# Attention and a gated feed-forward on one core: the reciprocals of the softmax sums go through DRAM and a broadcasting DMA instead of 64-fold copies and transpositions

## The chip, the cores and the metric

The kernel runs on one core of a Trainium2 chip. Its time is the device time of one execution, in microseconds (us). A core has a matrix engine (PE, with its weight loads shown apart as PEld), a vector engine (DVE), a scalar engine (ACT), a general engine (POOL), a queue engine that here only issues transfers (SP), and 16 DMA engines. The engines run side by side; each takes its own instructions in order and waits on semaphores for the others.

## The reference, cut to what matters

```python
def _attn_ref(q, k, v):                       # (8, 8, 576, 64) each
    scores = np.matmul(q, k.transpose(0, 1, 3, 2)) / np.sqrt(64)
    mask = (pos[:, None] // 64) >= (pos[None, :] // 64)
    scores = np.where(mask, scores, -1e9)
    scores = scores - np.max(scores, axis=-1, keepdims=True)
    attn = np.exp(scores)
    attn = attn / (np.sum(attn, axis=-1, keepdims=True) + 1e-09)
    return np.matmul(attn, v)

def _moe_ref(x, w_in, w_out):                 # x: 4608 x 512, from the 8 heads of each batch
    h = x @ w_in                              # 4608 x 2048
    sp = np.maximum(h, 0.0) + np.log1p(np.exp(-np.abs(h)))
    return (h * erf(sp)) @ w_out              # 4608 x 512
```

## The kernel before, in words

There are 8 batches of 8 heads, 64 heads in all, numbered n. Accuracy is kept by splitting operands into a high and a low part, so that nearly every product is three matrix multiplications.

**Attention.** The main loop has one step for each head and four more (`for n in range(N + 4)`). A step emits, merged evenly: the loads of head n+3 (`load_qk`: a load to `st` on SP, a load into `qk` on POOL's queue, two copies from SBUF to SBUF on SP, then two subtractions on POOL, L312 and L313, for the low parts); the row maxima of head n+2 (`maxes`, L324 on PE, L327 on DVE, then a transposition and L356 on ACT); the probabilities of head n (`probs`, L370 and L371 on PE, L375 and L381 on ACT, L382 on DVE); and for each pair of heads the unnormalised outputs `usb` and the sums `rs` (`pv`, L414 to L440). In the second step of every four, v of the next four heads is loaded; in the third it is split (`prep_v`, L276 to L292).

**Normalising.** Two pairs of heads, four heads, make a quad; there are 16 quads, two to a batch. For each quad `normalise` turns the sums so that queries lie on partitions (L453, six small products into `rt`), takes the reciprocals (L454, `ri`), and then, for each of the two pairs, copies each reciprocal 64 times along a row (L462, `rw`, on ACT), transposes these rows back on PE (L467, five products for a pair, into two PSUM banks `rb`) and multiplies `usb` by them on DVE (L469). The product is split into two parts (L470 on ACT, L471 on POOL) and written to `x_d` in DRAM by SP (L472). All of it is emitted in one step of the main loop, the one with n = 1 modulo 4.

**Feed-forward.** d_ff is 16 chunks of 128. The first six (`F1`) go through `moe1` while attention runs: units of two chunks over 256 tokens, up (L154), the gate (L123 to L137) and down (L164). They read `x_d` back (L187) when a batch is ready (`ready_at`). What is left of them follows after attention, and then come the other ten chunks over 512 tokens at a time. The weights come as the words of float64 and are converted by DVE, ACT and POOL (L94 to L108).

**Order.** The kernel is written in this order, but a scheduler takes each instruction by its place in the program as a priority and issues it on its engine where its own model finds the operands ready. So multiplications of `moe1`, which stand late in the program, fill places between those of attention. Until the first `x_d` is read, each step also emits ten products that nobody reads (`warm`, L510).

PSUM has eight banks. `bank` gives four of them in turn to scores, probabilities, sums, outputs and the reciprocals (`ps_a`) once the feed-forward has begun.

## Time and profile before

| | us |
|---|---|
| median of three runs | 1399.85 |
| lowest and highest of them | 1387.88, 1400.71 |
| the profiled execution, first to last instruction | 1407.0 |
| PE busy in it | 1273.8 (91%) |
| PE loading weights | 1026.1 (73%) |
| DVE busy | 1013.9 (72%) |
| ACT busy | 793.2 (56%) |
| POOL busy | 602.1 (43%) |

The profiled execution is 0.5% longer than the median of the runs. Busy time is the time in which an engine had an instruction under way; "idle before" is the time that an engine stood before the instructions of a group, with what ended it. The profile names instructions by line and by what they write and read. Windows of time (from the span's start) give the busy time of each engine in a stretch, the clock that PE was granted (1.00 is full speed) and the share of the 16 DMA engines. Attention lasts from the start to about 760 us, what is left of the first six chunks to about 850 us, and the other ten chunks to the end.

### The profile page before, as it was taken

The page shows a single profiled execution, that of the slowest core. Times are in us where ns is not written, and L with a number is a line of the kernel's source. Part 1 is how long each engine was busy: PE and PEld are TensorE (multiplying, and loading weights), DVE is VectorE, ACT ScalarE, POOL GpSimd, SP SyncE. Part 2 cuts the span into 40 slices and gives each one's busy share as a digit, 9 for nine tenths or more (in the row PEclk, how much of TensorE's full clock was granted, in tenths as well). Part 3 has the DMA queues.
Part 4 walks back from the last instruction along what each step waited for, and adds up shares of the span by engine and source line. Part 5 has one row for each costly group of instructions (what it writes and reads, how often), then busy time and mean ns, then how long its engine had stood idle before and what let it go on. Part 6 is the DMA issues. An engine that isn't in the chain of part 4 may idle for free. (4 is left out here: it accounts for less than half of the span.)

```text
span 1407.0 us, 21952 instructions
## 1 busy us (share of the span) xinstructions
PE 1273.8 (91%) x8198; PEld 1026.1 (73%) x8198; DVE 1013.9 (72%) x1525; ACT 793.2 (56%) x1493; POOL 602.1 (43%) x454
## 2 busy tenths in 40 slices
PE   3798789989899898999889898779999999999998
PEld 1455567777777787777777787568888888888887
DVE  5768997788878788788697648996555555564654
ACT  1456566667666676667567455544444454445453
POOL 3757665445554554544445424562222222222221
PEclk9879899999999999999999899899999999999999
DMA  8557655757657576566623542302211311321110
GB/s 228 135 125 204 173 156 137 185 154 193 179 129 207 146 196 175 152 161 177 174 81 137 188 164 95 130 0 78 102 60 68 113 60 60 108 72 61 60 61 30
DMA packets 89370, 179.95 MB, mean 128 GB/s; under 512 B 8540, under 2 KB 27292, under 8 KB 89264
## 3 DMA queue, kind: packets, MB, share of 16 engines
q1 hardware_dynamic: 79280, 159.41, 38.1%
q0 software_dynamic: 9344, 18.97, 6.1%
q8 instruction: 65, 1.06, 0.3%
q10 hardware_dynamic: 640, 0.17, 0.1%
q14 instruction: 41, 0.34, 0.1%
HBM read 112.29 MB, written 37.75 MB: 107 GB/s over the span
## 5 line engine op out<-in xcount | busy, mean ns | idle before, releaser
L130 DVE SCALAR_TENSOR_TENSOR m_r<-m_r 128x512 f32<-128x512 f32 x288 | 232.9, 809 | 229.3 <-ACT m_r L128 225.8
L137 POOL TENSOR_TENSOR m_gl<-m_r,m_gh 128x512 fp32r<-128x512 f32 x144 | 195.5, 1357 | 443.7 <-ACT m_gh L136 359.2
L136 ACT CAST m_gh<-m_r 128x512 fp32r<-128x512 f32 x144 | 89.2, 619 | 251.9 <-DVE m_r L135 251.7
L154 PE MATMUL m_h<-xh,whi 128*128 128x256 f32 (+1 forms) x648 | 213.3, 329 | 17.3 <-DVE m_r L135 17.3
L128 ACT ACTIVATE m_r<-m_r,c 128x512 f32<-128x512 f32 x288 | 207.9, 722 | 11.0 <-ACT m_r L128 0.4
L154 PE MATMUL m_h<-xl,whi 128*128 128x256 f32 (+1 forms) x648 | 211.1, 326 | 0.3 <-DMA xl<-x_d 0.3
L154 PE MATMUL m_h<-xh,wlo 128*128 128x256 f32 (+1 forms) x648 | 211.1, 326 | 0.0
L327 DVE TENSOR_REDUCE mx<-s 64x1 f32<-64x288 f32 (+4 forms) x384 | 167.9, 468 | 56.4 <-PE s L324 53.9
L375 ACT ACTIVATE p<-t 128x288 f32<-128x288 f32 (+4 forms) x384 | 143.1, 388 | 97.9 <-PE t L371 76.2
L164 PE MATMUL o<-whi,m_gh 128*128 128x512 f32 x432 | 173.8, 403 | 6.7 <-ACT ob L209 4.3
L164 PE MATMUL o<-wlo,m_gh 128*128 128x512 f32 x432 | 173.8, 402 | 0.0
L382 DVE TENSOR_TENSOR pl<-p,ph 128x832 f16<-128x832 f32 (+1 forms) x128 | 158.5, 1240 | 18.0 <-ACT ph L381 17.8
L312 POOL TENSOR_TENSOR qk<-st,qk 64x576 fp32r<-64x576 f32 x64 | 103.2, 1613 | 157.5 <-PE s L324 55.9
L154 PEld LDWEIGHTS m_h<-xh,whi 128*128 128x128 f32 x648 | 126.6, 195 | 37.8 <-DVE m_r L135 21.9
L164 PE MATMUL o<-whi,m_gl 128*128 128x512 f32 x432 | 153.0, 402 | 0.2 <-POOL m_gl L137 0.2
L370 PE MATMUL t<-qk 69*128 69x288 f32 (+4 forms) x384 | 136.0, 355 | 12.6 <-DVE mx L327 7.0
L324 PE MATMUL s<-qk 68*128 68x256 f32 (+3 forms) x384 | 126.6, 362 | 14.3 <-DVE mx L327 8.7
L313 POOL TENSOR_TENSOR qk<-st,qk 64x576 fp32r<-64x576 f32 x64 | 111.3, 1739 | 65.5 <-DMA qk<-qk 61.7
L154 PEld LDWEIGHTS m_h<-xl,whi 128*128 128x128 f32 x648 | 126.5, 195 | 15.8 <-DMA xl<-x_d 0.6
L154 PEld LDWEIGHTS m_h<-xh,wlo 128*128 128x128 f32 x648 | 126.9, 196 | 9.4
L371 PE MATMUL t<-qk 128*128 128x288 f32 (+4 forms) x384 | 129.8, 339 | 0.0
L123 ACT ACTIVATE m_r<-m_h,c 128x512 f32<-128x512 f32 x144 | 98.8, 686 | 50.5 <-PE m_h L154 48.7
(84 smaller groups left out, 2499.1 us busy)
## 6 DMA issues: line engine op xcount, KB each, us to landing
st<-qk SPq DMA_DIRECT2D x64, 288.0 KB
qk<-qk POOLq DMA_DIRECT2D x64, 288.0 KB, 4.6
qk<-qk SPq DMA_DIRECT2D x64, 288.0 KB
x_d<-xs SPq DMA_DIRECT2D x32, 576.0 KB
raw<-w SPq DMA_DIRECT2D x32, 512.0 KB
v<-v SPq DMA_DIRECT2D x16, 640.0 KB
qk<-qk SPq DMA_DIRECT2D x64, 144.0 KB
xh<-x_d SPq DMA_DIRECT2D x18, 512.0 KB
```

Of the source, the lines that this page charges most:

```text
L128: nc.scalar.activation(r, regs[o[1]], AF.Square, bias=const(pp[1]), scale=pp[0])
L130: nc.vector.scalar_tensor_tensor(out=r, in0=regs[o[1]], scalar=pp[0], in1=regs[o[2]], op0=ALU.add, op1=ALU.mult)
L137: nc.gpsimd.tensor_tensor(out=gl, in0=g, in1=f32(gh), op=ALU.subtract)
L154: nc.tensor.matmul(h[:, k, :], lhsT=a[:, 0, sl], rhs=x[:, cc, :], start=cc == 0 and i == 0, stop=cc == NCC - 1 and i == 2)
L164: nc.tensor.matmul(o[c], lhsT=a[:, sl], rhs=b_[:, 1, :], start=first and k == 0 and not lo and b_ is whi, stop=last and k == nu - 1 and lo)
L313: nc.gpsimd.tensor_tensor(out=t[D:, 1, :], in0=st[D:, :], in1=f32(t[D:, 1, :]), op=ALU.subtract)
L324: nc.tensor.matmul(dst[:r, :w_], lhsT=qh[:K, i * P : i * P + r], rhs=kh[:K, k0 : k0 + w_], start=True, stop=True)
L327: nc.vector.tensor_reduce(out=mx[:r, col : col + 1], in_=src, axis=AX.X, op=ALU.max, negate=True)
L370: nc.tensor.matmul(s[:kk, :w_], lhsT=kh[:K, ks], rhs=qh[:K, q0 : q0 + w_], start=True, stop=False)
L371: nc.tensor.matmul(s[:kk, :w_], lhsT=klh[:, ks], rhs=qhl[:, q0 : q0 + w_], start=False, stop=True)
L375: nc.scalar.activation(p32s[part][:kk, c : c + w_ - skip], s[:kk, skip:w_], AF.Exp, scale=SCALE)
L382: nc.vector.tensor_tensor(out=pl, in0=p, in1=ph, op=ALU.subtract)
```

## The change

The reciprocals are taken in two instructions of 12 columns, in an order in which the transposed rows are whole lines of a head (`ri` is pair, head, part, tile). One transposition on PE then gives 24 rows of 128 (`rr`), which ACT copies into SBUF, into a buffer of the tag `mt` that the row maxima use too, and SP writes to a small tensor `r_d` in DRAM. For each pair, two DMAs on SP read one row of 576 each and write it to 64 partitions (`rb`, now in SBUF, with one buffer for both pairs); one multiplication on DVE of 128x576 takes the place of two that read PSUM.

`normalise` returns two lists. The first (sums, reciprocals, rows) stays in the step with n = 1 modulo 4; the second (broadcast, product, split, write) goes to the next step, the one with `prep_v`. `ready_at` moves by a step as well, so that ten more `warm` products are issued (120 for 110).

```diff
+    r_d = tc.dram_tile((B * H // 4, 2, 2, 2 * 384), F32, name="r_d")
...
-            ri = apool.tile([P, 2, 3, 2, 2], F32, tag="ri", name=f"ri{nm}")
+            ri = apool.tile([P, 2, 2, 2, 3], F32, tag="ri", name=f"ri{nm}")
...
-                nc.vector.reciprocal(out=ri.rearrange("p a b c d -> p (a b c d)"), in_=pt[:, :24])
+                for pp in range(2):
+                    nc.vector.reciprocal(out=ri[:, pp], in_=pt[:, 12 * pp : 12 * pp + 12].rearrange("p (i f d) -> p d f i", i=3, f=2))
+
+            def rows():
+                pr = bank(f"rr{nm}")
+                nc.tensor.transpose(out=pr[:24, :P], in_=ri.rearrange("p a b c d -> p (a b c d)"), identity=ident)
+                rr = apool.tile([24, P], F32, tag="mt", name=f"rr_{nm}")
+                nc.scalar.copy(rr, pr[:24, :P])
+                nc.sync.dma_start(r_d[b * NQ + qd].rearrange("a b (t p) -> (a b t) p", p=P), rr)
...
             def m(pp):
+                rb = apool.tile([P, S], F32, tag="rb", name=f"rb{nm}_{pp}", bufs=1)
+                for hd in range(2):
+                    nc.sync.dma_start(rb[64 * hd : 64 * hd + 64, :], r_d[b * NQ + qd, pp, hd : hd + 1, :S].broadcast_to([64, S]))
...
-                rw = apool.tile([P, 5, 2, D], F32, tag="rw", name=f"rw{nm}_{pp}", bufs=1)
-                for hf, k in enumerate((3, 2)):
-                    nc.scalar.copy(rw[:, 3 * hf : 3 * hf + k], ri[:, pp, :k, hf, :].unsqueeze(3).broadcast_to([P, k, 2, D]))
-                for hf, (q0, q1) in enumerate(((0, 384), (384, 576))):
-                    rb = bank(f"rb{nm}_{pp}_{hf}")
-                    for i in range(q0 // P, (q1 + P - 1) // P):
-                        r = min(P, S - i * P)
-                        nc.tensor.transpose(out=rb[:, i * P - q0 : i * P - q0 + r],
-                                            in_=rw[:r, i].rearrange("p a b -> p (a b)"), identity=ident[:r, :r])
-                    nc.vector.tensor_tensor(out=x32[:, q0:q1], in0=usbs[pp][:, q0:q1], in1=rb[:, : q1 - q0], op=ALU.mult)
+                nc.vector.tensor_tensor(out=x32, in0=usbs[pp], in1=rb, op=ALU.mult)
...
-            return [a, lambda: m(0), lambda: m(1)]
+            return [a, rows], [lambda: m(0), lambda: m(1)]
...
+            if n in outs:
+                lists.append((outs.pop(n), 0.1, 0.8))
             if n in normals:
...
+                lists.append((late("norm", steps[0]), 0.6, 1))
+                outs[n + 1] = late("norm", steps[1])
                 if q_ == NQ - 1:
-                    ready_at[n + 1] = (b + 1) * S // T
+                    ready_at[n + 2] = (b + 1) * S // T
```

Line numbers after the change are higher by one, and from `normalise` on by more: the two reciprocals are L456, the transposition L461, the copy L463, the write L464, the broadcasts L470, the product L473, the split L474 and L475, the write of `x_d` L476.

**DVE, the eighth quad** (the second of batch 3; in the profile of before its reciprocal starts at 409.73 us). The names: `xs` is the normalised output of a pair, `mx` the row maxima, `pl` the low part of the probabilities, `vs`, `vsb` and `vl` belong to the next quad's v. Before:

```order
L454 RECIPROCAL ri_1_4405<-rt_1_4480 128x24
L327 TENSOR_REDUCE mx_123<-s_35_1_4488 64x1
L382 TENSOR_TENSOR pl_33_4477<-p_0_113,ph_33_4476 128x832
L352 TENSOR_TENSOR mx_123<-mx_123 64x1
L469 TENSOR_TENSOR xs_1_0_4495<-usb_4056,rb_1_0_0_4499 128x384
L469 TENSOR_TENSOR xs_1_0_4495<-usb_4056,rb_1_0_1_4504 128x192
L469 TENSOR_TENSOR xs_1_1_4525<-usb_4289,rb_1_1_0_4529 128x384
L382 TENSOR_TENSOR pl_33_4522<-p_1_114,ph_33_4521 128x768
L469 TENSOR_TENSOR xs_1_1_4525<-usb_4289,rb_1_1_1_4534 128x192
```

In the changed kernel, from the end of the same step of the main loop on (the reciprocals stand ten rows ahead of the first row shown):

```order
L281 TENSOR_REDUCE vs_1_4502<-vt_1_4500 1x1
L282 TENSOR_SCALAR vs_1_4502<-vs_1_4502 1x1
L283 RECIPROCAL vs_1_4502<-vs_1_4502 1x1
L287 COPY vsb_1_4508<-vb_1_4506 128x2
L473 TENSOR_TENSOR xs_1_0_4486<-usb_3980,rb_1_0_4483 128x576
L328 TENSOR_REDUCE mx_123<-s_36_0_4525 64x1
L328 TENSOR_REDUCE mx_123<-s_36_1_4544 64x1
L293 SCALAR_TENSOR_TENSOR vl_1_4511<-v_4_1_4342,vsb_1_4508,vh_1_4510 128x1280
L353 TENSOR_TENSOR mx_123<-mx_123 64x1
```

The products moved from right behind the reciprocals to the middle of `prep_v` of the next quad, ahead of the last maximum (L353) of a later head. From the second reciprocal to the first product there are now 12 instructions of DVE, and from the first product to the second 9; over all quads the counts between are 11 to 22 and 7 to 15.

**SP, the same quad.** `st` and `qk` are loads of later heads, `part_d` is a store of the feed-forward. Before:

```order
L306 DMA st_4771<-qk 128x576
L472 DMA x_d<-xs_1_0_4495 128x2x576
L308 DMA qk_95<-qk_95 64x1152
L472 DMA x_d<-xs_1_1_4525 128x2x576
L309 DMA qk_95<-qk_95 64x576
```

After:

```order
L464 DMA r_d<-rr_1_4437 24x128
L307 DMA st_4700<-qk 128x576
L470 DMA rb_1_0_4483<-r_d 64x576 x2
L211 DMA part_d<-ob_1_8689 128x512
L309 DMA qk_96<-qk_96 64x1152
L310 DMA qk_96<-qk_96 64x576
L470 DMA rb_1_1_4536<-r_d 64x576
L476 DMA x_d<-xs_1_0_4486 128x2x576
L470 DMA rb_1_1_4536<-r_d 64x576
L270 DMA v_5_0_4815<-v 128x1280
```

The write of the reciprocals, the four broadcasts and the loads of other work now stand in one queue: the first broadcast behind a load of `st`, which waits for POOL, and the second half of the second pair's broadcast behind the write of the first pair's output. On PE, 1283 of the 4104 products of the feed-forward stood ahead of attention's last score product before, and 1152 do now.

More of the change, by code (lines that the diff above doesn't have):

```diff
@@ L472, in m @@
                 nc.sync.dma_start(x_d[:, c * P : (c + 1) * P, b * S : (b + 1) * S].rearrange("s p t -> p s t"), f32(xs))
-            return [a, lambda: m(0), lambda: m(1)]
+            return [a, rows], [lambda: m(0), lambda: m(1)]
         vs, prs, usbs = {}, {}, {}
-        normals, ready_at, ready = {}, {}, 0
+        normals, outs, ready_at, ready = {}, {}, {}, 0
         for n in range(NB - 1):
@@ L543, in tile_attention_moe @@
                 b, q_ = divmod(qd, NQ)
-                lists.append((late("norm", normalise(b, q_, [usbs.pop(2 * qd), usbs.pop(2 * qd + 1)], [rss[2 * qd % 3], rss[(2 * qd + 1) % 3]])), 0.6, 1))
+                steps = normalise(b, q_, [usbs.pop(2 * qd), usbs.pop(2 * qd + 1)], [rss[2 * qd % 3], rss[(2 * qd + 1) % 3]])
+                lists.append((late("norm", steps[0]), 0.6, 1))
+                outs[n + 1] = late("norm", steps[1])
                 if q_ == NQ - 1:
-                    ready_at[n + 1] = (b + 1) * S // T
+                    ready_at[n + 2] = (b + 1) * S // T
             ready = ready_at.get(n, ready)
```

## The prediction

> **What bounds the kernel now.** I read first the mean clock and the span, then the busy time of each engine in stretches of the span: 100 us at the start, two quads in the middle of attention, the stretch behind attention and one of the last stage.
>
> ```profile
> core 0: 1407.0 us, clock 0.951
> core 0: us, PE busy (x) PEld busy (x) DVE busy (x) ACT busy (x) POOL busy (x), PEclk, DMA share, GB/s
> 100.00:150.00 50.00, 40.74 (x320) 25.79 (x318) 44.28 (x75) 30.21 (x66) 36.74 (x26) 0.95 0.67 182
> 150.00:200.00 50.00, 42.65 (x332) 33.44 (x333) 46.95 (x67) 30.08 (x63) 34.53 (x22) 0.84 0.58 157
> 398.00:442.00 44.00, 41.06 (x349) 34.44 (x349) 34.49 (x56) 29.92 (x63) 23.87 (x17) 0.96 0.59 160
> 442.00:486.00 44.00, 39.05 (x334) 31.87 (x334) 35.05 (x58) 29.02 (x61) 21.92 (x16) 0.96 0.66 168
> 900.00:950.00 50.00, 34.21 (x129) 26.86 (x129) 48.62 (x55) 24.29 (x40) 29.63 (x19) 0.86 0.06 21
> 1000.00:1050.00 50.00, 50.00 (x223) 41.40 (x222) 27.63 (x40) 24.64 (x38) 12.41 (x10) 1.00 0.25 85
> ```
>
> The change touches attention only, to about 760 us. Up to 200 us DVE bounds it (44 to 47 of 50 us; it converts weights there), and PE has time to spare. From then on PE is busy 89% to 93% of a quad of 44 us, and DVE 78% to 80%. The last stage is PE alone. So three of the 16 quads lie where time saved on PE is worth nothing, and 13 where it is worth nearly all of itself, as long as nothing makes PE wait longer.
>
> Where PE does wait in attention shows in steps of 11 us of the eighth quad, and in two waits of the ninth:
>
> ```profile
> 398.00:409.00 11.00, 10.81 (x113) 8.72 (x113) 8.96 (x15) 8.37 (x19) 7.38 (x5) 1.00 0.39 88
> 409.00:420.00 11.00, 10.60 (x80) 9.23 (x80) 7.55 (x13) 8.03 (x17) 4.85 (x4) 1.00 0.57 140
> 420.00:431.00 11.00, 9.65 (x77) 8.04 (x75) 8.66 (x14) 5.45 (x12) 6.89 (x5) 0.84 0.65 201
> 473.01 0.28 PE L354 MATMUL mt<-ident,mx 128*5 128x128 f32 x1 [2.78 <-DVE mx L352]
> 478.60 1.49 DVE L276 TENSOR_REDUCE vm<-v 128x1 f32<-128x1280 f32 x1 [3.69 <-DMA v<-v]
> 481.94 0.35 PE L324 MATMUL s<-qk 68*64 68x288 f32 x1 [1.34 <-DVE mx L327]
> ```
>
> The step that normalises (409 to 420) is nearly full on PE; the next one, with the preparation of v, is the weak one, with PE standing 1.35 us and a clock of 0.84. The ninth quad shows how: PE stood 2.78 us for a maximum that DVE was late with. And DVE stood 3.69 us for a transfer, of which PE, which has work queued ahead, felt 1.34 us.
>
> **The change, part by part.** The groups that go, and those that give the new durations:
>
> ```profile
> L467 PE MATMUL rb<-ident,rw 128*128 128x128 f32 (+1 forms) x160 | 29.1, 284 | 0.2
> L469 DVE TENSOR_TENSOR xs<-usb,rb 128x384 f32<-128x384 f32 x64 | 27.1, 449 | 17.4 <-issue 9.2 <-PE rb L467 5.7 <-POOL qk L313 1.2
> L462 ACT COPY rw<-ri 128x384 f32<-128x384 f32 x64 | 26.9, 455 | 11.0 <-PE rb L467 10.9
> L454 DVE RECIPROCAL ri<-rt 128x24 f32<-128x24 f32 x16 | 4.9, 305 | 15.0 <-PE rt L453 15.0
> L130 DVE SCALAR_TENSOR_TENSOR m_r<-m_r 128x512 f32<-128x512 f32 x288 | 232.9, 809 | 229.3 <-ACT m_r L128 225.8
> L282 DVE RECIPROCAL vs<-vs 1x1 f32<-1x1 f32 x16 | 2.4, 148 | 0.3
> L356 ACT CAST mt<-mt 5x128 fp32r<-5x128 f32 x64 | 16.1, 251 | 53.0 <-PE mt L354 52.6
> L510 PE MATMUL warm<-id 128*128 128x512 f16 x110 | 39.2, 453 | 9.1 <-DVE mx L327 9.1
> 145.00:156.00 11.00, 5.94 (x45) 3.65 (x44) 11.00 (x20) 5.63 (x11) 9.06 (x6) 0.68 0.60 180
> L370 PE MATMUL t<-qk 69*128 69x288 f32 (+4 forms) x384 | 136.0, 355 | 12.6 <-DVE mx L327 7.0 <-ACT mt L356 4.3 <-DVE vsb L286 0.9
> ```
>
> *PE.* 160 transpositions are worth 29.1 us, 0.18 us each where they follow one another; 16 come back, 2.9 us. Of the difference, 26.2 us, 13/16 count: 21.3 us gained. Bounds: 26.2 where the first quads count too, nothing where another engine decides.
>
> *The warm products.* Ten more at 39.2/110 = 0.36 us are 3.6 us. They fall into the step where the feed-forward started before, about 145 to 156 us, where PE was busy 5.94 of 11 us and DVE all of it: nothing, and 3.6 us if that cover is gone.
>
> *ACT and PSUM.* ACT loses 26.9 us and gains 16 x 0.25 = 4.0 us. It isn't the bound, but PE stood 4.3 us for its copy of the maxima (L356), which queues behind these copies among others; and a quad takes two banks where it took five. I take 4 us as gained, between 0 and 10.
>
> *DVE.* The product now reads two operands from SBUF. The nearest row of that kind is L130, 809 ns for 512 columns, so 0.91 us for 576, 29 us for 32 against 27.1. The reciprocals of 12 columns lie between 148 and 305 ns, say 0.22: 7.0 against 4.9 us. Together 4 us more in the whole run. What matters is the place: the products move out of the step at 409 us into the weak one, where the order puts the first ahead of the very maximum that PE stood for. Fully felt that is 0.91 x 13 = 12 us; but the step before becomes lighter by the same. I take half, 6 us, between -6 and 12.
>
> *Issue and traffic.* SP issues five transfers more in a quad, at 0.4 to 0.6 us each (L472 and L309, below); it mostly waits, so the time to issue costs nothing. The broadcasts move 64 x 144 KB, 9.4 MB:
>
> ```profile
> q1 hardware_dynamic: 79280, 159.41, 38.1%
> ```
>
> At that rate it is 2.2% of the span on 16 engines, in attention some 0.05 beside a share of 0.59 to 0.67. That leaves room.
>
> *The arrival of the reciprocals.* Two products of DVE, which waited for PE, now wait for DMAs, and behind them in DVE's queue stand the maxima, for which PE waits. No row shows a write to DRAM followed by a read. What rows there are on transfers that an engine waits for, or that stand in SP's queue:
>
> ```profile
> L313 POOL TENSOR_TENSOR qk<-st,qk 64x576 fp32r<-64x576 f32 x64 | 111.3, 1739 | 65.5 <-DMA qk<-qk 61.7 <-DMA part_d<-ob 1.0 <-ACT p L375 0.7
>   DMA qk<-qk: 61.7, 34
> 447.38 0.59 SPq L309 DMA_DIRECT2D qk<-qk  x1
> 451.74 1.40 POOL L313 TENSOR_TENSOR qk<-st,qk 64x576 fp32r<-64x576 f32 x1 [2.29 <-DMA qk<-qk]
> 411.62 0.59 SPq L309 DMA_DIRECT2D qk<-qk  x1
> 414.27 1.43 POOL L313 TENSOR_TENSOR qk<-st,qk 64x576 fp32r<-64x576 f32 x1 [1.70 <-DMA qk<-qk]
> SPq L306 <- POOL qk L313: 173.7, 49, 6.0
> 409.73 0.31 DVE L454 RECIPROCAL ri<-rt 128x24 f32<-128x24 f32 x1 [1.24 <-PE rt L453]
> 424.65 0.15 DVE L286 COPY vsb<-vb 128x2 f32<-128x2 f32 x1
> 412.51 0.80 DVE L469 TENSOR_TENSOR xs<-usb,rb 128x384 f32<-128x384 f32 x2
> 417.81 0.38 SPq L472 DMA_DIRECT2D x_d<-xs x1
> ```
>
> L309 copies 144 KB to 64 partitions, the shape of one broadcast: 2.65 us from issue to its reader at 411.62, 4.36 at 447.38. The scheduler placed that reader where it thought the data would be there, and over 64 of them it stood 61.7 us, 0.96 us each. The new products are placed by the same scheduler: three legs in a quad (write, first broadcast, second broadcast) at 0.96 us are 2.9 us of DVE standing. Of such standing PE felt 1.34/3.69 = 0.36, so 1.04 us in a quad, and over 13 quads 13.6 us. Bounds: nothing, if the legs fit in their cover; and 35 us (the second rival).
>
> How near the cover is: in the traced quad the copy after which the first product now stands starts 14.9 us after the reciprocals; without the four products (0.45 us each, L469) and the three instructions of the gate that stood between (0.81 us or more each, L130), 9 to 11 us are left. The path is two reciprocals 0.4, a transposition 0.3 and a copy 0.25 (L467, L356), some 1.5 in the queues of PE and ACT (an estimate: L356 waited 52.6/64 = 0.8 us for PE each time), a write of 2.65 to 4.36, 0.6 to issue and a read of the same: 8.4 to 11.8 us. It is about even, so half the quads wait.
>
> The Trainium skill (DMA: Bandwidth & Descriptors, "Anatomy of one DMA") speaks against such a round trip: a transfer has a fixed cost of about 2.0 us, most of it the receipt from the target, longest where that is HBM, and bytes/436 GB/s on top. By it the two legs would be 2.0 and 2.3 us, an estimate, shorter than the rows say; the sum would then lose the 13.6 us. The rows above show more than that formula for 144 KB, so I go by the rows.
>
> *The order.* 131 products of the feed-forward leave attention for the stretch behind it, some 45 us at about 0.35 us. PE is the bound in both, so this is no gain or loss; but quads get shorter with the same work of attention for DVE.
>
> *The sum:* -21.3 - 4 + 6 + 13.6 = -5.7 us. The profiled span becomes 1401.3 us; it stood to the median as 1407.0 to 1399.85, so 1401.3 x 0.9949 = 1394 us.
>
> **The rivals.** *The transfers land in time.* For it: only 34 of the 64 readers of L309's data waited, and between reciprocals and first product stand 11 to 22 instructions of DVE. Then the 13.6 us fall away and the move of the products costs 3 in place of 6: -21.3 - 4 + 3 = -22, 1385 x 0.9949 = 1378 us. The page's fixed cost, quoted above, would give this case.
>
> *SP's queue delays both products, and it gets slower.* Place: the second half of the second pair's broadcast stands behind the write of the first pair's output, which waits for POOL. Before, from the product's end (413.31) to that write's issue (417.81) went 4.5 us; with two issues and 4.36 us of landing that is 9.7 us, and in the order only 7 to 15 instructions of DVE lie between the two products. The first broadcast stands in many quads behind a load of `st`, and these waited for POOL 173.7/49 = 3.5 us each. If both products stand 3.7 us, PE feels 2 x 1.34 = 2.7 us in a quad, 35 us in all: -21.3 - 4 + 6 + 35 = +16, 1423 x 0.9949 = 1416 us. It breaks even at 1.5 us in a quad that PE feels, and decides for slower by 1% at 2.5. Against it: SP has done its waits in before without much harm to PE.
>
> The Trainium skill (TensorE: Matmul & The Clock Gate, "Part 1: The HAM clock gate") says that PE's clock halves after an idle window of about 3.4 us and comes back after a busy one. By it, stands that stay below that cost no more than themselves. The trace is stricter: after the 2.78 us at 473 us the next products took 0.47 us for 0.30, so this rival could reach 1430.
>
> ```profile
> 474.41 0.48 PE L414 MATMUL u<-ph,vh 128*64 128x320 f16 x2
> 404.02 0.30 PE L414 MATMUL u<-pl,vh 128*64 128x320 f16 x2
> ```
>
> *DVE becomes the bound.* With some 3 us less of feed-forward and 1.6 us less of transpositions in a quad, its 44 us become 39.4, and DVE's 35 us lose 0.8 with the gate: 87%. At 89% to 94% (100 to 200 us) PE's share was 81% to 85%. If PE's share in attention falls from 91% to 89%, 2% of some 650 us, 13 us, join the sum: 1407 us.
>
> **How the numbers follow.** A measurement of this kernel tells about 1%, 14 us, from no change. The forecast, part of the gain given back (1386 to 1402): 0.36. The transfers in time, 1378 (1364 to 1386): 0.34, all of it faster. SP's queue, 1416 (1403 to 1430): 0.22, which I count as slower. DVE the bound, 1407 (1400 to 1420): 0.08, half of it slower. So faster 0.34, within 1% 0.36 + 0.04 = 0.40, slower 0.22 + 0.04 = 0.26. The likeliest is 1394. The range of 8 in 10 leaves off the outer ends of the first and second rival: 1368 to 1424.
>
> **What would show it.** PE's busy time in attention without the 29 us of `rb`; DVE's idle time before the products (L473), put down to `rb`'s transfers: near 45 us (16 x 2.9) by the forecast, below 15 in the first rival, above 100 in the second; PE's idle time before L325 and L355 put down to DVE, up by some 14 us; the clock in the step with the preparation of v, 0.84 or less. The prediction is wrong if these products hardly wait and the time still does not fall, or if the time moves outside attention, behind 760 us.

## The result

| | before | after |
|---|---|---|
| device time, median (lowest to highest) | 1400.28 us (1387.88 to 1401.56) | 1435.32 us (1432.63 to 1443.81) |
| span of the profiled execution | 1407.0 us | 1430.9 us |
| granted clock, profiled | 0.951 | 0.939 |
| PE busy, profiled | 1273.8 us | 1273.3 us |
| span less PE busy | 133.2 us | 157.6 us |

The changed kernel takes 1.0278 times as long (95% interval 1.0234 to 1.0322). It is slower, by 35 us in the medians and 24 us in the two profiled spans. The prediction was 1394 us, with a range to 1424. A few executions of the kernels below were over 1.5% longer than the fastest of their kernel; they count in no ratio and in no mean of the clock.

The head of the page of after, and the queue that carries the new transfers:

```profile
core 0: 1430.9 us, clock 0.939
PE 1273.3 (89%) x8064; PEld 1021.0 (71%) x8064; DVE 1014.8 (71%) x1509; ACT 775.5 (54%) x1445; POOL 616.1 (43%) x454
q1 hardware_dynamic: 84976, 169.05, 40.5%
```

PE is as long busy as before, though 29.1 us of transpositions have left it and 16 short ones have come. Part of this is the clock: the span times what is missing in the clock is 1407.0 x 0.049 = 68.9 us before and 1430.9 x 0.061 = 87.3 us after. Less that, PE's busy time is 1204.9 us before and 1186.0 after. So 19 us of work are gone as they should be; 18 came back as a lower clock and 24 as time in which PE stands. That is the 24 us of the span. (The clock is a mean over the whole span, so a part of what it takes falls where PE stands anyway; the three numbers say where to look, not more.)

Where in time: the first three rows are three stretches of attention in before, the last three the same quads in after. The columns are the stretch and its length, the busy time of PE, PEld, DVE, ACT and POOL (instructions in brackets), PE's clock, the share of the DMA engines and GB/s.

```profile
189.00:410.00 221.00, 202.44 (x1723) 165.96 (x1722) 182.49 (x293) 149.85 (x316) 112.82 (x85) 0.96 0.63 165
410.00:672.00 262.00, 241.99 (x2070) 198.34 (x2068) 210.93 (x346) 180.95 (x380) 132.36 (x99) 0.97 0.65 172
672.00:768.00 96.00, 86.12 (x700) 70.26 (x701) 74.92 (x114) 64.03 (x133) 50.26 (x33) 0.95 0.42 126
```

```profile
189.00:411.00 222.00, 196.85 (x1670) 160.52 (x1670) 180.19 (x288) 144.30 (x304) 120.53 (x85) 0.95 0.69 178
411.00:684.00 273.00, 240.62 (x1972) 194.00 (x1972) 205.87 (x334) 170.05 (x356) 136.25 (x97) 0.93 0.68 173
684.00:787.00 103.00, 92.67 (x701) 73.62 (x700) 84.70 (x119) 65.14 (x129) 55.74 (x35) 0.89 0.47 145
```

To the eighth quad's reciprocals (410 and 411 us) the two keep pace. From there on, after takes 11 us longer for the same quads, with 98 instructions of PE fewer in them and the clock at 0.93 in place of 0.97; PE's share falls from 92% to 88%. The last quad's reciprocals start at 758 us before and 764 after, and what is left of the span behind them is 649 us before and 667 after: the 131 products of the feed-forward that left attention are done there, and attention did not get shorter in exchange.

Who waited for whom, before and then after (the total, how often, the longest):

```profile
PE mt L354 <- DVE mx L352: 26.4, 23, 2.8
DVE mx L327 <- PE s L324: 53.9, 82, 2.9
SPq L306 <- POOL qk L313: 200.2, 55, 6.1
```

```profile
PE mt L355 <- DVE mx L353: 40.9, 29, 4.2
DVE mx L328 <- PE s L325: 84.2, 95, 6.6
DVE xs L473 <- DMA rb<-r_d: 23.8, 13, 4.4
ACT xs L474 <- DVE xs L473: 30.5, 22, 3.7
SPq L307 <- POOL qk L314: 150.3, 53, 7.5
```

DVE stands 23.8 us for the broadcasts (`rb`), at 13 of 32 products. SP's loads of `st`, ahead of the broadcasts in its queue, waited 150.3 us for POOL, less than the 200.2 of before (the 173.7 in the prediction leave out the first 90 us; after has 122.8 there). PE stands 14.5 us longer for the maxima, and DVE 30 us longer for the scores out of which it takes them: both ends of one loop, PE, DVE, PE, wait more for one another.

One quad, the twelfth, in instructions (start, duration, and in brackets how long the engine stood before it and for what):

```profile
588.94 0.32 DVE L456 RECIPROCAL ri<-rt 128x12 f32<-128x12 f32 x2 [1.34 <-PE rt L454]
589.98 0.24 ACT L463 COPY rr<-rr 24x128 f32<-24x128 f32 x1
591.35 0.90 SPq L464 DMA_DIRECT2D r_d<-rr  x1
595.65 0.35 SPq L307 DMA_DIRECT2D st<-qk  x1
596.10 1.11 SPq L470 DMA_DIRECT2D rb<-r_d  x2
601.68 1.06 DVE L473 TENSOR_TENSOR xs<-usb,rb 128x576 f32<-128x576 f32 x1 [4.38 <-DMA rb<-r_d]
602.66 0.14 DVE L283 RECIPROCAL vs<-vs 1x1 f32<-1x1 f32 x1
602.77 0.67 ACT L474 CAST xs<-xs 128x576 fp32r<-128x576 f32 x1 [3.74 <-DVE xs L473]
602.86 0.38 PE L285 MATMUL vb<-vs,onesrow 1*128 1x2 f32 x2 [3.94 <-DVE vs L283]
```

From the reciprocals to the product go 12.7 us, more than the 8.4 to 11.8 of the estimate. The broadcasts were issued 4.75 us behind the write, the load of `st` ahead of them, and the product began 4.5 us after the second had been issued. DVE stood 4.38 us, and behind the product in its queue was the reciprocal of `prep_v`, so PE stood 3.94 us, 0.9 of it and not 0.36. The clock in the four microseconds of the stand and in the four behind it:

```profile
598.00:602.00 4.00, 0.92 (x7) 0.66 (x5) 0.32 (x1) 1.03 (x2) 1.27 (x1) 1.00 0.72 155
602.00:606.00 4.00, 3.14 (x40) 2.33 (x40) 3.38 (x7) 2.04 (x2) 3.92 (x4) 0.74 0.69 172
```

1.00, then 0.74. The Trainium skill (TensorE: Matmul & The Clock Gate, "Part 1: The HAM clock gate") puts the idle window at about 3.4 us; this stand was longer and the clock fell, so row and page agree here. The prediction's 2.78 us at 473 us, shorter than that, had slower products behind it too (0.47 us for 0.30).

### The profile page after: what moved, and what is told of

Read it like the earlier page. It is cut to its first block, busy times and chain, and to the rows that moved or that the text cites. A ratio compares the mean times of both kernels' runs of the same rounds, so it can differ in the third digit from the quotient of the medians.

```text
span 1430.9 us, 21735 instructions
## 1 busy us (share of the span) xinstructions
PE 1273.3 (89%) x8064; PEld 1021.0 (71%) x8064; DVE 1014.8 (71%) x1509; ACT 775.5 (54%) x1445; POOL 616.1 (43%) x454
## 4 chain that ended last, share of the span: by engine, by line
PE 57%; DVE 23%; DMA 8%; issue 3%; ACT 2%; POOL 1%; SPq 0%; DVEq 0%; ACTq 0%; POOLq 0%
PE o L165 21%; PE m_h L155 21%; DVE m_r L131 6%; DMA rb<-r_d 4%; PE u L415 4%; DVE pl L383 3%; PE s L325 3%; DVE mx L328 3%; PE t L372 2%; PE t L371 2%; DMA qk<-qk 2%; DVE xs L473 2%; DVE mx L353 2%; DVE sq L103 2%; PE rt L454 1%
## 5 line engine op out<-in xcount | busy, mean ns | idle before, releaser
L138 POOL TENSOR_TENSOR m_gl<-m_r,m_gh 128x512 fp32r<-128x512 f32 x144 | 199.6, 1386 | 439.5 <-ACT m_gh L137 423.2
L383 DVE TENSOR_TENSOR pl<-p,ph 128x832 f16<-128x832 f32 (+1 forms) x128 | 149.2, 1166 | 13.7 <-ACT ph L382 13.5
L371 PE MATMUL t<-qk 69*128 69x288 f32 (+4 forms) x384 | 140.0, 365 | 19.9 <-DVE mx L328 8.8
```

What stands on the lines that cost most here:

```text
L138: nc.gpsimd.tensor_tensor(out=gl, in0=g, in1=f32(gh), op=ALU.subtract)
L371: nc.tensor.matmul(s[:kk, :w_], lhsT=kh[:K, ks], rhs=qh[:K, q0 : q0 + w_], start=True, stop=False)
L383: nc.vector.tensor_tensor(out=pl, in0=p, in1=ph, op=ALU.subtract)
```

## The experiments

Each kernel was timed beside the kernel before. "Lost" is, averaged over a kernel's timed runs, span x (1 - clock); "PE stands" is the profiled span less PE's busy time; "filling" is the feed-forward products that the order puts ahead of attention's last score product.

| kernel | median us | ratio to before (95%) | lost us | PE stands us | filling |
|---|---|---|---|---|---|
| before | 1400 | 1 | 63 | 133 | 1283 |
| after | 1435 | 1.0278 (1.0234 to 1.0322) | 95 | 158 | 1152 |
| e1_same_step | 1436 | 1.0275 (1.0194 to 1.0356) | 97 | 158 | 1145 |
| e1_ready_source | 1434 | 1.0264 (1.0179 to 1.0349) | 99 | 152 | 1070 |
| e1_before_split | 1420 | 1.0149 (1.0067 to 1.0231) | 66 | 132 | 1144 |
| e1_before_free | 1408 | 1.0074 (1.0038 to 1.0111) | 86 | 132 | 1118 |
| e2_before_hoist | 1413 | 1.0090 (1.0052 to 1.0128) | 68 | 136 | 1359 |
| e2_before_late | 1410 | 1.0057 (1.0025 to 1.0090) | 73 | 132 | 1351 |
| e2_free_traffic | 1403 | 1.0030 (0.9998 to 1.0063) | 73 | 135 | 1140 |
| e2_early_rb | 1433 | 1.0228 (1.0168 to 1.0288) | 91 | 158 | 1202 |
| e3_free_rows | 1405 | 1.0020 (0.9980 to 1.0060) | 78 | 141 | 1099 |
| e3_split_free | 1412 | 1.0085 (1.0047 to 1.0123) | 85 | 138 | 1002 |
| e3_same_ready | 1409 | 1.0083 (1.0039 to 1.0127) | 82 | 137 | 1061 |
| e3_act_write | 1423 | 1.0161 (1.0093 to 1.0229) | 79 | 157 | 1128 |
| e4_same_unread | 1409 | 1.0052 (1.0015 to 1.0090) | 78 | 142 | 1110 |
| e4_after_unread | 1428 | 1.0200 (1.0122 to 1.0279) | 89 | 146 | 1070 |
| e4_same_pool | 1439 | 1.0262 (1.0193 to 1.0331) | 96 | 160 | 1159 |
| e4_after_pool | 1471 | 1.0489 (1.0423 to 1.0555) | 109 | 184 | 1125 |
| e5_split_rows | 1431 | 1.0234 (1.0168 to 1.0300) | 100 | 144 | 1070 |
| e5_split_traffic | 1413 | 1.0099 (1.0060 to 1.0138) | 77 | 151 | 1066 |

### One part at a time: the later step, the dependence, the work that goes

**Round trip whole, products in the reciprocals' own step** (e1_same_step; of after):

```diff
-                lists.append((late("norm", steps[0]), 0.6, 1))
-                outs[n + 1] = late("norm", steps[1])
+                lists.append((late("norm", steps[0] + steps[1]), 0.6, 1))
...
-                    ready_at[n + 2] = (b + 1) * S // T
+                    ready_at[n + 1] = (b + 1) * S // T
```

> The changed kernel with the broadcasts and products back in the step of the reciprocals, and x_d ready a step earlier, as before. If the arrival of the transfers is the cause, DVE has less work between reciprocals and products to cover them: its standing at the products grows from 23.8 us to 40 or more, and the time is 1440 us or more. If the place of the products (in the step that prepares v, with the later start of the feed-forward) is the cause, most of the loss goes: 1400 to 1412 us.

1436 us: the same as after. Taking the move back wins nothing; the round trip in the old place costs as much, though not for the same reason, as the later groups show.

**The broadcasts read an input that is there from the start** (e1_ready_source; of after):

```diff
-                    nc.sync.dma_start(rb[64 * hd : 64 * hd + 64, :], r_d[b * NQ + qd, pp, hd : hd + 1, :S].broadcast_to([64, S]))
+                    nc.sync.dma_start(rb[64 * hd : 64 * hd + 64, :], qk[b, 4 * qd + 2 * pp + hd, 0:1, :].broadcast_to([64, S]))
```

> The changed kernel with the broadcasts reading rows of an input that lies ready in DRAM, so that the products use wrong factors and nothing waits for the write of the reciprocals; all transfers, their sizes and engines stay. If the arrival is the cause, DVE hardly stands at the products and the time falls to 1400 us or below. If place and order are the cause, it stays at 1425 to 1445 us.

1434 us, though the products had no data to wait for. But this kernel differs in more than that: with nothing to wait for, the scheduler drew the broadcasts far forward, the first to 5.9 us, and the filling fell to 1070. It speaks against the wait as the whole cause in the later step; it doesn't tell what the cause is there (see the last group).

**The copies and transpositions as before, products in the next step** (e1_before_split; of before):

```diff
-            return [a, lambda: m(0), lambda: m(1)]
+            return [a], [lambda: m(0), lambda: m(1)]
...
-        normals, ready_at, ready = {}, {}, 0
+        normals, outs, ready_at, ready = {}, {}, {}, 0
...
+            if n in outs:
+                lists.append((outs.pop(n), 0.1, 0.8))
...
-                lists.append((late("norm", normalise(b, q_, [usbs.pop(2 * qd), usbs.pop(2 * qd + 1)], [rss[2 * qd % 3], rss[(2 * qd + 1) % 3]])), 0.6, 1))
+                steps = normalise(b, q_, [usbs.pop(2 * qd), usbs.pop(2 * qd + 1)], [rss[2 * qd % 3], rss[(2 * qd + 1) % 3]])
+                lists.append((late("norm", steps[0]), 0.6, 1))
+                outs[n + 1] = late("norm", steps[1])
...
-                    ready_at[n + 1] = (b + 1) * S // T
+                    ready_at[n + 2] = (b + 1) * S // T
```

> The kernel before, with copies and transpositions, but with the second half of the normalisation in the next step and x_d ready a step later, as the change has it. If the arrival of the transfers is the cause, this stays at 1395 to 1410 us. If the place and the order of the work are the cause, it is slow without any round trip: 1420 to 1445 us.

1420 us: the later step with the later start of the feed-forward costs 20 us, with the same work on every engine but for ten more warm products (120, at 0.36 us 3.6 us). PE stands no longer than before (132 us) and the clock loses no more (66 us for 63). What is left to tell them apart is the order, and with it where the feed-forward is done: in the profiled run the last quad's reciprocals come at 744 in place of 758 us, but with 139 products more behind them the rest takes 672 in place of 649 us, and PE is busy 1283.6 us for 1273.8.

**The work that goes, with nothing in its place** (e1_before_free; of before: the copies, transpositions and products with `rb` are out, and the unnormalised output is multiplied by itself):

```diff
-                rw = apool.tile([P, 5, 2, D], F32, tag="rw", name=f"rw{nm}_{pp}", bufs=1)
...
-                    nc.vector.tensor_tensor(out=x32[:, q0:q1], in0=usbs[pp][:, q0:q1], in1=rb[:, : q1 - q0], op=ALU.mult)
+                nc.vector.tensor_tensor(out=x32, in0=usbs[pp], in1=usbs[pp], op=ALU.mult)
```

> The kernel before with copies and transpositions left out and nothing in their place (the products multiply the outputs by themselves): less work on PE, ACT and the PSUM banks, no round trip, no shift. If the work on PE bounds attention, 21 to 26 us are saved: 1374 to 1380 us. The scheduler puts only 1145 products of the feed-forward ahead of the last score product here, 1283 before and 1152 in the changed kernel; if this thinner filling is the cause, the time is 1400 us or more although this kernel does least.

(The filling of 1145 that the expectation names is e1_same_step's; this kernel's is 1118.) This was the surprise of the study. All that the change could save is saved here, at no price, and the time is 1408 us: not less than before, but 0.7% more (the profiled run is one of its longer ones, 1418). Two of its waits; then attention and the rest of the span, cut at the last quad's reciprocals, in before and in this kernel:

```profile
PE mt L354 <- DVE mx L352: 31.5, 23, 4.4
DVE mx L327 <- PE s L324: 71.3, 94, 2.8
```

```profile
0.00:758.00 758.00, 661.47 (x5384) 518.21 (x5385) 605.70 (x974) 479.88 (x1012) 405.91 (x312) 0.93 0.62 165
758.00:1407.00 649.00, 612.29 (x2816) 507.94 (x2815) 408.20 (x552) 313.30 (x482) 196.21 (x142) 0.97 0.25 85
```

```profile
0.00:744.00 744.00, 646.32 (x5066) 495.75 (x5067) 597.88 (x926) 444.32 (x929) 406.13 (x308) 0.89 0.62 164
744.00:1416.50 672.50, 637.94 (x2974) 530.25 (x2973) 422.26 (x568) 326.82 (x500) 201.37 (x146) 0.97 0.25 86
```

Up to the last quad's reciprocals PE is busy 15 us less, and attention is 14 us shorter; PE stands there as long as before (97.7 us for 96.5). But the clock is 0.89 in place of 0.93, which is 82 us lost for 53 (744 x 0.11 and 758 x 0.07). At full clock some 44 us of PE's work have left attention, and 29 us of that went to the clock. Behind attention PE is busy 26 us longer and the rest takes 23.5 us more, for 165 products of the feed-forward that attention no longer holds. So attention does get shorter; a lower clock takes most of what it saves, and the products that it no longer holds take more than what is left. DVE stands 17 us longer for the scores.

### Is it the filling?

The feed-forward put further forward (e2_before_hoist), and only the start of its later tokens moved (e2_before_late); both of before.

```diff
-        PRIO = {"pv": -74, "w1": 400, "w2": -300}
+        PRIO = {"moe": -300, "pv": -74, "w1": 400, "w2": -300}
```

> The kernel before with the same work, but the feed-forward's steps moved 300 places ahead in the scheduler's priority: 1359 of its products stand ahead of the last score product, 1283 before, 1144 in the kernel that was split without a round trip (1420 us). If the filling of attention with the feed-forward sets the time at equal work (21 us for 139 products, 0.15 us each), this gains 76 x 0.15 = 11 us: 1387 us. If the filling says nothing, 1395 to 1402 us.

```diff
-                    ready_at[n + 1] = (b + 1) * S // T
+                    ready_at[n + 2] = (b + 1) * S // T
```

> The kernel before with x_d declared ready one step later and nothing else; ten more warm products. The scheduler's order then has 1351 products of the feed-forward ahead of the last score product. If the later start is what costs in the change, this is slower, 1405 us or more. If the filling sets the time, it gains 68 x 0.15 = 10 us: 1388 us.

More filling than the kernel before in both, and both slower, 1413 and 1410 us. The theory that after is slow because less of the feed-forward lies in attention falls as a rule for the time: 1359 and 1351 products give more time than 1283, and 1002 (e3_split_free) gives the same 1412. Moved forward, the products save 14 to 15 us behind attention (635 and 634 us for 649) and lengthen it by 12 to 20 (770 and 778 us for 758). What the two do show is that another order of nearly the same work costs 8 to 13 us. What they don't test is a kernel without the transpositions: no run leaves those out and keeps the filling at 1283.

### What the parts cost in the old step

**The traffic alone** (e2_free_traffic): e1_before_free, with the 64 broadcasts of an input row into a tile that nobody reads.

```diff
+                rb = apool.tile([P, S], F32, tag="rb", name=f"rb{nm}_{pp}", bufs=1)
+                for hd in range(2):
+                    nc.sync.dma_start(rb[64 * hd : 64 * hd + 64, :], qk[b, 4 * qd + 2 * pp + hd, 0:1, :].broadcast_to([64, S]))
```

> The kernel without copies, transpositions and round trip (1408 us), with the 64 broadcasts put back, from an input and into a tile that nobody reads: the traffic and the places in SP's queue alone. The filling is 1140, 1118 without them. If traffic and queue cost, 1420 to 1436 us; if only the waiting for the reciprocals costs, 1402 to 1412 us.

1403 us. The 9.4 MB and SP's issues cost nothing that shows.

**The rows and the write alone** (e3_free_rows): e1_same_step with two reciprocals, transposition, copy and write as they are, but no broadcasts and the product of `usb` by itself.

```diff
-                rb = apool.tile([P, S], F32, tag="rb", name=f"rb{nm}_{pp}", bufs=1)
-                for hd in range(2):
-                    nc.sync.dma_start(rb[64 * hd : 64 * hd + 64, :], r_d[b * NQ + qd, pp, hd : hd + 1, :S].broadcast_to([64, S]))
...
-                nc.vector.tensor_tensor(out=x32, in0=usbs[pp], in1=rb, op=ALU.mult)
+                nc.vector.tensor_tensor(out=x32, in0=usbs[pp], in1=usbs[pp], op=ALU.mult)
```

> The kernel without copies, transpositions and broadcasts (1408 us, PE idle 132 us), with the first part of the round trip put back, in the same step: two reciprocals, the transposition into rows, the copy by ACT into a tile of mt, the write to r_d by SP. Nothing reads r_d. All kernels with this part had 152 to 158 us of PE idle time, all without it 132 to 136. If this part is what costs, 1425 to 1440 us; if not, 1400 to 1412 us.

1405 us: nothing either.

**All of it, with data that is there** (e3_same_ready): e1_same_step whose broadcasts read the input row, as in e1_ready_source. **All of it, with products that don't look** (e4_same_unread): e1_same_step, the product of `usb` by itself, write and broadcasts as they were.

```diff
-                nc.vector.tensor_tensor(out=x32, in0=usbs[pp], in1=rb, op=ALU.mult)
+                nc.vector.tensor_tensor(out=x32, in0=usbs[pp], in1=usbs[pp], op=ALU.mult)
```

> Reciprocals, rows, write and broadcasts in one step, the broadcasts from an input that lies ready: the first part and the traffic, without a wait for data and without the split. If the first part costs, 1425 to 1440 us as with the wait (1436); if the wait for the data costs, 1400 to 1412 us.

> Round trip in the step of the reciprocals (1436 us), but the products multiply the outputs by themselves and read no rb: SP's queue still stands for the write, DVE, ACT and POOL behind it wait for no transfer. If DVE's standing is the cost, it falls to 1403 to 1412 us; if SP's queue is, it stays at 1425 to 1440 us.

1409 us in both, against 1436 with the dependence. This is the price of the products' dependence on the round trip: 27 us. The groups of the maxima's transposition and of the cast behind the product, in e1_same_step:

```profile
L355 PE MATMUL mt<-ident,mx 128*5 128x128 f32 x64 | 18.9, 295 | 45.1 <-DVE mx L353 44.8
L474 ACT CAST xs<-xs 128x576 fp32r<-128x576 f32 x32 | 21.4, 670 | 32.4 <-DVE xs L473 31.9 <-DMA v<-v 0.2
  DMA rb<-r_d: 11.3, 11
```

and in e4_same_unread:

```profile
L355 PE MATMUL mt<-ident,mx 128*5 128x128 f32 x64 | 18.6, 290 | 25.9 <-DVE mx L353 25.8
L474 ACT CAST xs<-xs 128x576 fp32r<-128x576 f32 x32 | 21.4, 667 | 1.2 <-DVE xs L473 1.1
```

DVE stood only 11.3 us for the transfers, as the last of the three rows of e1_same_step says, but ACT stood 31 us more in front of the cast, and PE 19 us more for the maxima. One caution: the scheduler, which knows of the wait, orders the two kernels differently (about one PE instruction in ten stands elsewhere), and the profiled run of e1_same_step is its longest (1446 us); so the 27 us hold both the wait and what the order makes of it.

### Is SP's queue the carrier?

**The write off SP's queue** (e3_act_write; of after), **write and broadcasts off it** (e4_same_pool of e1_same_step, e4_after_pool of after):

```diff
-                nc.sync.dma_start(r_d[b * NQ + qd].rearrange("a b (t p) -> (a b t) p", p=P), rr)
+                nc.scalar.dma_start(r_d[b * NQ + qd].rearrange("a b (t p) -> (a b t) p", p=P), rr)
```

```diff
-                    nc.sync.dma_start(rb[64 * hd : 64 * hd + 64, :], r_d[b * NQ + qd, pp, hd : hd + 1, :S].broadcast_to([64, S]))
+                    nc.gpsimd.dma_start(rb[64 * hd : 64 * hd + 64, :], r_d[b * NQ + qd, pp, hd : hd + 1, :S].broadcast_to([64, S]))
```

> The changed kernel with the write of the reciprocals on ACT's queue instead of SP's, so that SP does not stand for ACT's copy (32.5 us in the changed kernel) and the loads behind it go at once. If that standing is the cost, 1405 to 1420 us; if not, 1428 to 1440 us.

> Round trip in the step of the reciprocals, with the write on ACT's queue and the broadcasts on POOL's: SP's queue is as without a round trip. If SP's queue is the cost, 1403 to 1412 us; if DVE's standing is, 1425 us or more, and POOL, which now stands for the write, may add to it.

> The changed kernel with the write on ACT's queue and the broadcasts on POOL's. If SP's queue is the cost, 1405 to 1415 us (with the write alone on ACT's queue it was 1423); if DVE's standing is, 1420 us or more.

DVE's waits for the broadcasts, in e3_act_write and then in the two others:

```profile
DVE xs L473 <- DMA rb<-r_d: 7.8, 5, 2.8
```

```profile
  DMA rb<-r_d: 28.1, 18
```

```profile
  DMA rb<-r_d: 61.9, 19
```

With the write on ACT's queue DVE stands a third as long as in after and the time falls to 1423; that is 12 us of the 35, the two intervals just missing one another, and the only edit that helped the round trip in after's place. With the broadcasts on POOL's queue too, it is no better in the old step (1439 us for 1436) and worse in after's place (1471, where DVE stands 61.9 us for them). In the old step e4_same_unread tells: SP still stands 27.9 us there for ACT's copy of the rows (37.4 in e1_same_step) and 145.7 for POOL at the loads of `st` (137.7), and the time is 1409. So there SP's queue by itself costs nothing that shows; what costs is that the products depend on the transfers. In after's place this is not settled: e4_after_unread, below, keeps SP's stand for the copy (31.8 us, 34.3 in after), reads no `rb`, and takes the 1428 us that its expectation gave for SP's queue; and e3_act_write changes SP's queue and DVE's stand at once.

**The broadcasts right behind the write** (e2_early_rb; of after, straight into the tile of the product):

```diff
                 nc.sync.dma_start(r_d[b * NQ + qd].rearrange("a b (t p) -> (a b t) p", p=P), rr)
+                for pp in range(2):
+                    xs = apool.tile([P, 2, S], F32R, tag="xs", name=f"xs_{nm}_{pp}")
+                    for hd in range(2):
+                        nc.sync.dma_start(f32(xs[64 * hd : 64 * hd + 64, 1, :]), r_d[b * NQ + qd, pp, hd : hd + 1, :S].broadcast_to([64, S]))
+                    xss.append(xs)
...
-                nc.vector.tensor_tensor(out=x32, in0=usbs[pp], in1=rb, op=ALU.mult)
+                nc.vector.tensor_tensor(out=x32, in0=usbs[pp], in1=x32, op=ALU.mult)
```

> The changed kernel with the broadcasts issued right behind the write of the reciprocals, into the tile of the output (two buffers), and the products in the next step, so that DVE finds them there. The filling is 1202, 1152 in the changed kernel. If the waiting for the transfers costs, DVE stands less than 8 us at the products and the time falls to 1410 to 1420 us; of that 50 x 0.15 = 8 us would be the filling's. If only order and filling count, 1427 us.

1433 us. DVE still stood 14.6 us in nine products, and nothing was won.

### The changed kernel's own place, the next step

**No round trip** (e3_split_free), **the broadcasts unread** (e5_split_traffic), **rows and write only** (e5_split_rows), **everything, unread** (e4_after_unread). All are after with the product of `usb` by itself; what else is left out stands in the name. The edits are those of the same-step kernels, on after (the broadcasts of e5_split_traffic read the input row); e3_split_free and e5_split_traffic also drop `rows`:

```diff
-            return [a, rows], [lambda: m(0), lambda: m(1)]
+            return [a], [lambda: m(0), lambda: m(1)]
```

> The same without that part, but with the products in the next step and x_d ready a step later, as the change places them. With copies and transpositions this split cost 20 us (1420). If the place of the products costs, 1425 us or more here too; if only the transfers' part costs, 1400 to 1412 us.

> Products in the next step without reading anything (1412 us), with the broadcasts put back, from an input and into a tile that nobody reads, no write. If the traffic makes the difference in this place, 1424 to 1434 us; if not, 1405 to 1415 us, and if both stay there, the difference is the order that the scheduler makes of them together, or a spread of such orders.

> Products in the next step without reading anything (1412 us), with the reciprocals in two, rows, copy and write put back, no broadcasts. If the write, which stands in SP's queue, makes the difference in this place, 1424 to 1434 us; if not, 1405 to 1415 us.

> The changed kernel (1435 us) with products that read no rb. If DVE's standing is the cost, 1403 to 1415 us (split without any round trip: 1412); if SP's queue is, 1425 to 1440 us.

1412 without round trip, 1413 with the broadcasts, 1431 with rows and write, 1428 with all of it unread, 1435 with the reading. So here the wait is worth some 7 us at most by the medians, not clear of noise (the intervals of the last two overlap), and 15 to 19 come in with a transposition, a copy and a 12 KB write, which cost nothing in the old step (1405). **Left open:** the three kernels with rows but no wait of the products, e5_split_rows, e4_after_unread and e1_ready_source, have almost the same order on PE (under 2% of the instructions stand elsewhere) and lie at 1428 to 1434; the two without rows have other orders (about 10% stand elsewhere, between the two of them also) and lie at 1412 and 1413. Whether the rows, the write in SP's queue or the order that the scheduler makes once they are there costs these 15 to 19 us, no run separates.

No kernel of the study is faster than the one before.

## Why the prediction was wrong, step by step

The forecast of 1394 us lies 41 us below the measured 1435. Measured in the old step, the first of the terms below is off by 24 to 35 us, and the arrival of the reciprocals by 13.

**"13 of 16 quads, 21.3 us gained" (PE): this step failed.** It counted the time that PE saves in attention as time that the kernel saves. Seven kernels without the transpositions and without a wait for the round trip (e1_before_free, e2_free_traffic, e3_free_rows, e3_same_ready, e4_same_unread, e3_split_free, e5_split_traffic) took 1403 to 1413 us, none less than before. The term was worth nothing, or 0.2% to 1.0% (3 to 14 us) of the other sign. What stands in its place: PE's work at full clock did fall, by 13 to 20 us and not 26 (from 1205 us to between 1185 and 1192 in the profiled runs of these seven), and attention did get shorter: the last quad's reciprocals come at 721 to 744 us in them, at 758 before. But the rest then takes 667 to 692 us in place of 649, with a filling of 1002 to 1140 for 1283, and over the whole span the clock loses 73 to 86 us for 63 and PE stands 132 to 151 for 133. That the saving is lost is shown; why the clock is granted lower with less work on PE is not, and how much of the loss the thinner filling makes is open too.

**"131 products leave attention: no gain or loss" failed with it.** It supposes that attention gets shorter by what leaves it. In after it got 6 us longer and the rest 18 us. The sign named for this, time behind 760 us, came true. The price of 0.35 us each was wrong as well: that is how long one product lasts, and PE's products overlap. In before, two that follow one another start 0.12 us apart, and the 18 us of after are 0.14 us for each of the 131:

```profile
478.28 0.28 PE L154 MATMUL m_h<-xl,whi 128*128 128x256 f32 x1
478.40 0.28 PE L154 MATMUL m_h<-xh,wlo 128*128 128x256 f32 x1
```

**"ACT and PSUM, 4 us gained"** can't be told from the same nothing: e1_before_free has this relief too.

**"The products move, 6 us" was too small.** e1_before_split, where they move together with the later start of the feed-forward, costs 20 us (ratio 1.0067 to 1.0231); the later start alone costs 8 (e2_before_late). With the move, attention holds 139 products less, and the rest is 23 us longer in the profiled run. The product itself was rightly sized, a median of 0.81 us for 0.91, the reciprocals at 222 ns for 0.22:

```profile
L473 DVE TENSOR_TENSOR xs<-usb,rb x32: 740/810/1951, 103.4 to 783.4; 128x576 f32<-128x576 f32 x32
L456 DVE RECIPROCAL ri<-rt x32: 161/222/233, 93.6 to 765.1; 128x12 f32<-128x12 f32 x32
```

**"The arrival of the reciprocals, 13.6 us": the waits were over-sized and their effect under-sized.** DVE stood 23.8 us, not 45 (one product in 2.5, not each of three legs at 0.96 us). But 0.36 as PE's share of a stand came from one load of v with work queued ahead on PE. The products stand ahead of what the loop needs next (`prep_v`'s reciprocal, the maxima, ACT's cast), and in the twelfth quad the share was 0.9. In the old step the dependence is worth 27 us for 11.3 that DVE stands. In after's own place the same subtraction gives 7, beside the 15 to 19 that are open. The forecast sign at L355, "up by some 14 us", was met with 14.5; that DVE's own wait for PE's scores would grow by 30 had no term in the sum.

**Issue and traffic at nothing: right.** 64 broadcasts cost nothing measurable (e2_free_traffic 1403, e5_split_traffic 1413 for 1412), at 9.64 MB more on queue q1 in after. The ten warm products were never run alone.

**The rivals.** "The transfers land in time, 1378" would have been wrong even if they had: e3_same_ready is that case in the old step, 1409, and e1_ready_source in after's, 1434. "SP's queue, 1416", with its range to 1430, came nearest in time, but by luck: it rests on DVE standing above 100 us at the products, and DVE stood 23.8, less than the forecast's 45. That SP's queue carries the loss is refuted for the old step and open for after's place. "DVE becomes the bound, 1407" is near to what the seven kernels give, but not as it was put: in after DVE is busy 470.8 of the 598 us from 189 to 787 us, 79%, and was busy 468.3 of 579 before, 81%: it is no more the bound than it was. What grew is what the engines wait for one another.

**The Trainium skill's price** (DMA: Bandwidth & Descriptors, "Anatomy of one DMA": 2.0 us and bytes/436 GB/s, fitted there for transfers that the general engine issues) gives 2.3 us for a broadcast of 144 KB, an estimate; the twelfth quad, where SP issues it, shows 4.5 us from issue to reader at a DMA share of 0.72. The trace doesn't agree, and by that price the forecast would have been the first rival's.

## What to carry to other kernels

Time saved on an engine that is 90% busy in a long stage is not yet time saved for the kernel: before counting it, leave the work out with nothing in its place and time that. Here this gave 1408 us for 1400 in one kernel, and 1403 to 1413 in all seven that had the work out. The duration of a row is no price either, where rows overlap: 131 products of 0.35 us took 18 us behind attention and not 45. Where a product of one engine's queue feeds the queue of the next, the price of a late operand is set by what stands behind it in that queue, so a short stand (11 us of DVE) can go with a loss larger than itself (27 us, order included). And in a kernel whose order comes out of a scheduler, any edit also buys a new order, which here was worth 8 to 20 us with nearly the same work.

## What was not expected of the hardware

- Less work on PE went with a lower granted clock: 63 us lost in the mean over the runs of before (66 to 73 in the three reordered kernels that keep the transpositions), 73 to 86 in the seven kernels without them whose products wait for nothing, 91 to 109 in five of the six with the wait (79 in e3_act_write), and 89 to 100 in the three of the later step that have the rows but no wait. What sets it is not shown.
- A write of 12 KB to DRAM and its reading back took 12.7 us from reciprocals to product in the twelfth quad, of which 4.75 us lay between the two issues and 4.5 between issue and use; no engine's busy time shows any of it.
